# Decode attention with a gated mixer on one core: a shorter TensorE program and a hand-ordered first part

## The chip, the core and the metric

One core of one Trainium2 chip. A core has TensorE (matrix products into PSUM), VectorE, ScalarE and GpSimd, and 16 DMA engines that move data between HBM and SBUF; SyncE issues most of the loads here. The metric is device time in microseconds of one launch, lower is better. Before the change, three runs gave a median of 193.45 us (193.33 to 193.55).

## What is computed

One token `x` of 512 numbers, 32 heads of 128, and for each head the last 4096 keys and values of a cache of 32768. Cut to what matters:

```python
xn = layernorm(x)
q  = (xn @ wq) per head                     # wq: 512 x 4096
p  = softmax(q . K[last 4096] * 128**-0.5)  # per head
s  = concat(p @ V[last 4096]) @ wo          # wo: 4096 x 512
h  = gelu(layernorm(xn) @ w1)
hs = concat(shifted h) @ w2                 # one token: every shift pads with zero, so hs = 0 @ w2
x1 = xn + hs
B  = x1 + gelu(layernorm(x1) @ w3) @ w4     # w3: 512 x 1376, w4: 1376 x 512
out = x + s * silu(B)
```

All is in bf16. K and V together are 67.1 MB, wq and wo 8.4 MB, w2 to w4 3.3 MB; the rest is small.

## The kernel before

**Groups.** Heads go in 8 groups of G = 4. A group's keys are one load of 128 partitions x 128 rows x 128 (4 MB): partition 4b + a holds rows of head a. A loop over steps s = 0 to 9 (from line 531) loads K of group s and V of group s - 2, computes scores of group s, the softmax of group s - 1 and the output of groups s - 2 and s - 3. K has three buffers, V has two, and the V buffers lie where the first part's weights were, so the first V load waits until those are read. Loads stand in a fixed order on SyncE's queue (`load`, line 75; w2, w3, w4, K0 in two halves, K1, K2, V0, K3, V1, and so on; last V7 in chunks of 64, 32 and 32 rows, then four heads of wo). wq and x are loaded by ScalarE's queue.

**Scores in two ways.** Of the 128 key rows per partition, `nd(g)` rows go to VectorE (`k_vector`, whose product is line 321 and whose sum is line 323): a product with the broadcast q, then a sum over 128, in four parts. The others go to TensorE: `k_turn` transposes pairs of rows as fp32 (line 339), ScalarE copies the result (line 342), `k_scores` multiplies by q (line 350). `nd` is 64 for groups 0 and 7 and 80 for the others.

**Softmax.** `sm_max`, `sm_turn`, `sm_exp` (lines 361 to 389) find each head's maximum and take the exponentials with a running sum on ScalarE. `sm_den` and `sm_rden` (lines 391 to 399) add the sums over the partitions by a product with ones and invert them, once for each group.

**Values.** `v_wide` (line 423) is 32 products for each group; `v_turn` and `v_add` turn and sum the result, `v_out` multiplies by the inverse denominator. The last group's final 32 rows go through `v_part` (line 458, products at 461). `ox_spread`, `ox_pick`, `y_wide` and `y_head` multiply the outputs by wo. `warm(n)` (line 504) issues n products of zeros whose result nobody reads.

**First part** (lines 182 to 280): layer norms, `hs` as 16 products with w2 (line 233), q as 32 products (line 208) with its broadcast `q_bc` and transposes, the input of the gelu in 20 products (line 252), three transposes of it (line 258), 15 products into `hr_ps` (line 270), and the gate `g_row`. Before the change a scheduler orders these instructions on each engine; from line 529 on, TensorE, VectorE and ScalarE are in a `manual_schedule`, which keeps them in the order of the program text. PSUM tiles of the tag `misc` have one buffer, of `sT` two, of `pt` three.

The lines of the main loop that the change touches:

```python
            elif s > 1:
                sm_den(s - 2)
                sm_rden(s - 2)
...
            y_wide(1, False)
            sm_den(NG - 2)
            sm_rden(NG - 2)
            y_wide(0, False)
            warm(3)
            v_wide(h, v)
            sm_den(NG - 1)
            sm_rden(NG - 1)
```

Of the kernel before, what the change touches and what calls it, by code (L numbers as in the profile page):

```python
# [8 lines left out]
P = 128  # L9
# [17 lines left out]
def kernel(  # L27
# [120 lines left out]
    def rows_open(ps):  # L148
        nc.tensor.matmul(ps[:], lhsT=zero_bf[:], rhs=ident_bf[:], start=True, stop=False,
                         skip_group_check=True)  # L150
# [30 lines left out]

    x_f = small.tile([P, KC], FP32, name="x_f")
# [16 lines left out]

    q_row = wts.tile([P, H // G, 2, Dh], BF16, name="q_row")  # L200
    q_bc = small.tile([P, H // G, Dh], BF16, name="q_bc")
    qr = [ps_tr.tile([P, 4, Dh], FP32, tag="pt", name="qr_ps") for _ in range(2)]
    for b in range(2):
        zeros(qr[b][:])
        for c in range(KC):
            wc = wq_sb[:, c, :].rearrange("p (g a d) -> p g a d", a=G, d=Dh)
            for a in range(G):
                nc.tensor.matmul(qr[b][32 * a:32 * a + 1], lhsT=xq_bf[:, c:c + 1], rhs=wc[:, 4 * b:4 * b + 4, a, :],  # L208
                                 start=False, stop=(c == KC - 1), skip_group_check=True)
    nc.scalar.copy(out=q_row[:, 0:4, 0, :], in_=qr[0][:])  # L210
    nc.vector.tensor_copy(out=q_row[:, 4:8, 0, :], in_=qr[1][:])  # L211
    for b in range(2):
        qb_ps = ps_tr.tile([P, 4, Dh], FP32, tag="pt", name="qb_ps")
        nc.tensor.matmul(qb_ps[:], lhsT=sel[:].rearrange("k b a -> k (b a)"), rhs=q_row[:, 4 * b:4 * b + 4, 0, :],
                         start=True, stop=True)
        nc.scalar.copy(out=q_bc[:, 4 * b:4 * b + 4, :], in_=qb_ps[:])
# [11 lines left out]
    shifted_bf = small.tile([P, KC], BF16, name="shifted_bf")  # L228
    nc.vector.memset(shifted_bf[:], 0.0)
    hs_ps = ps_misc.tile([P, KC], FP32, tag="misc", name="hs_ps")  # L230
    for j in range(KC):
        for c in range(KC):
            nc.tensor.matmul(hs_ps[:, j:j + 1], lhsT=w2_sb[:, c, j::4],
                             rhs=shifted_bf[:, c:c + 1], start=(c == 0), stop=(c == KC - 1))
    x1_f = small.tile([P, KC], FP32, name="x1_f")
    nc.vector.tensor_tensor(out=x1_f[:], in0=xn_f[:], in1=hs_ps[:], op=ALU.add)
    xc3, _, rstd3 = ln_stats(x1_f[:], "z3")
    z3_bf = small.tile([P, KC], BF16, name="z3_bf")
    nc.vector.tensor_scalar(out=z3_bf[:], in0=xc3[:], scalar1=rstd3[:], scalar2=None, op0=ALU.mult)

    xn_row = small.tile([P, P], FP32, name="xn_row")
    nc.vector.tensor_scalar(out=xn_row[:], in0=x_row[:], scalar1=negmean[:], scalar2=rstd[:],
                            op0=ALU.add, op1=ALU.mult)

    a_ps = ps_misc.tile([P, 3, P], FP32, tag="misc", name="a_ps")
    zeros(a_ps[:])
    for c in range(KC):
        wc = w3_sb[:, c, 0:10 * P].rearrange("p (q r) -> p r q", r=10)
        parts = [(j, a_ps[32 * j:32 * j + 1, :, :], wc[:, 3 * j:3 * j + 3, :]) for j in range(3)]
        parts += [(3, a_ps[96:97, 0, :], wc[:, 9, :]), (3, a_ps[96:97, 1, 0:96], w3_sb[:, c, 10 * P:F])]  # L250
        for j, dst, w in parts:
            nc.tensor.matmul(dst, lhsT=z3_bf[:, c:c + 1], rhs=w, start=False, stop=(c == KC - 1),
                             skip_group_check=True)
    a_row = wts.tile([P, 3, P], BF16, name="a_row")
    nc.scalar.activation(out=a_row[:], in_=a_ps[:], func=ACT.Gelu_apprx_tanh)  # L255
    at_ps = ps_misc.tile([P, 3, P], BF16, tag="misc", name="at_ps")
    for m in range(3):
        nc.tensor.transpose(at_ps[:, m, :], a_row[:, m, :], ident_bf[:])
    a_bf = small.tile([P, 3, 4], BF16, name="a_bf")
    nc.vector.tensor_copy(out=a_bf[:], in_=at_ps[:, :, 0:P:32])  # L260

    hr_ps = ps_misc.tile([P, KC, P], FP32, tag="misc", name="hr_ps")
    zeros(hr_ps[:])
    terms = [(shifted_bf[:, c:c + 1], w2_sb[:, c, :]) for c in range(KC)]
    for i in range(11):
        n = P if i < 10 else 96
        terms.append((a_bf[0:n, i % 3, i // 3:i // 3 + 1], w4_sb[0:n, i, :]))
    for i, (col, w) in enumerate(terms):
        r = 32 * (i % 4)
        nc.tensor.matmul(hr_ps[r:r + 1].rearrange("r j n -> r (j n)"), lhsT=col, rhs=w, start=False,  # L270
                         stop=(i >= len(terms) - 4), skip_group_check=True)
# [10 lines left out]

    make_masks(16)
    make_masks(8)
    make_masks(4)

    y_ps = ps_y.tile([P, P], FP32, name="y_ps")
    rows_open(y_ps)  # L290

# [16 lines left out]
    def nd(g):  # L308
        return 64 if g == 0 or g >= LATE else 80
# [68 lines left out]
    def sm_exp(g):  # L378
        s = st[g]
        mb_ps = ps_misc.tile([P, G], FP32, tag="misc", name="mb_ps")  # L380
        nc.tensor.matmul(mb_ps[:], lhsT=par_t[:].rearrange("k b a -> k (b a)"), rhs=md[:], start=True,  # L381
                         stop=True)
        mb = sm_pool.tile([P, G], FP32, tag="mb", name="mb")
        nc.scalar.copy(out=mb[:], in_=mb_ps[:])  # L384
        s["pT"] = sm_pool.tile([P, CP, G], BF16, tag="pT", name="pT")
        s["sum"] = sm_pool.tile([P, G], FP32, tag="sum", name="sum")
        for a in range(G):
            nc.scalar.activation(out=s["pT"][:, :, a], in_=s["S"][:], func=ACT.Exp, scale=scale,  # L388
                                 bias=mb[:, a:a + 1], accum_out=s["sum"][:, a:a + 1])

    def sm_den(g):
        s = st[g]
        s["den"] = ps_misc.tile([P, G], FP32, tag="misc", name="den_ps")
        nc.tensor.matmul(s["den"][:], lhsT=ones_f[:], rhs=s["sum"][:], start=True, stop=True)  # L394

    def sm_rden(g):
        s = st[g]
        s["rden"] = sm_pool.tile([P, G], FP32, tag="rden", name="rden")
        nc.vector.reciprocal(out=s["rden"][:], in_=s["den"][:])  # L399
# [64 lines left out]
    def v_out(g):  # L464
# [5 lines left out]
        if g >= NG - 5:  # L470
            nc.vector.tensor_tensor(out=o_blk[b][:, c:c + G], in0=st[g]["oT"][:], in1=st[g]["rden"][:],
                                    op=ALU.mult)
            return
# [48 lines left out]
    def y_head(h):  # L522
# [4 lines left out]
    region = tc.manual_schedule(engines={mybir.EngineType.PE, mybir.EngineType.DVE,  # L527
                                         mybir.EngineType.Activation})
    region.__enter__()
    v_pool = None  # L530
    for s in range(NG + LAG):
# [22 lines left out]
        if s < NG:  # L554
# [11 lines left out]
            if s == 7:  # L566
                v_turn(h - 1)
                v_add(h - 1)
                v_out(h - 1)
            elif s > 1:  # L570
                sm_den(s - 2)
                sm_rden(s - 2)
            elif s == 1:
                sm_max(0)
            k_vector(s, kn, 1)
            keys(2, 4)
            if s == 7:
                sm_den(h)
                sm_rden(h)
# [38 lines left out]
        elif s == NG:  # L618
# [4 lines left out]
            sm_den(NG - 2)  # L623
            sm_rden(NG - 2)
            y_wide(0, False)
            warm(3)
            v_wide(h, v)
            sm_den(NG - 1)
            sm_rden(NG - 1)
# [19 lines left out]
    region.__exit__(None, None, None)  # L649
    y = small.tile([P, P], FP32, name="y")  # L650
# [34 lines left out]
```

## Time and profile before

| what | value |
|---|---|
| time, median of three runs | 193.45 us |
| span of the profiled execution (first to last instruction) | 191.2 us |
| TensorE matmul busy | 116.4 us (61%), 1159 instructions |
| TensorE weight loads busy | 74.2 us (39%), 1159 instructions |
| VectorE busy | 150.9 us (79%) |
| ScalarE busy | 89.2 us (47%) |
| DMA | 79.02 MB, mean 413 GB/s |
| mean granted TensorE clock | 0.720 |

The page gives no total for the profiled execution beyond its span; the median of the runs is 2.25 us longer than the span. The span's rows of slices cut it into 40 equal pieces of 4.78 us: a digit is the busy share in tenths, PEclk the granted share of TensorE's clock. A load's "us to landing" runs from its issue, so it holds the time in the queue. In a timeline row the first number is the start in us from the span's start, the second how long the merged instructions took, and the bracket tells how long the engine was idle before and which event ended that. Matmul ends are modelled.

### The profile page before, as it was taken

How to read it: one execution, taken by the hardware profiler on the slowest of the kernel's cores; microseconds unless marked ns; L12 is line 12 of the kernel's file. 1: busy time of each engine (PE TensorE's matmuls, PEld its weight loads, DVE VectorE, ACT ScalarE, POOL GpSimd, SP SyncE). 2: the span in 40 equal slices, each digit the busy share in tenths (PEclk: the TensorE clock that was granted, in tenths of full speed). 3: DMA queues.
4: the chain of work that ended last, by engine and by line, in shares of the span. 5: the costliest groups of instructions: out<-in, count | busy, mean ns of one | idle time of the engine just before them, and what ended most of it. 6: DMA issues, size and time to landing. Idle time of an engine off the chain costs nothing.

```text
span 191.2 us, 2839 instructions
## 1 busy us (share of the span) xinstructions
PE 116.4 (61%) x1159; PEld 74.2 (39%) x1159; DVE 150.9 (79%) x175; ACT 89.2 (47%) x191; POOL 2.3 (1%) x11
## 2 busy tenths in 40 slices
PE   1653754989825368256845772680888189739762
PEld 0430222767614334143334441540763077313322
DVE  1660159979999999999999999999999999980111
ACT  2001370888794076427464564542475148733120
POOL 2110000000000000000000000000000000000000
PEclk9999695555755557955695588557567858975998
DMA  6999999999999999999999999999999998999990
GB/s 211 447 430 404 431 418 439 439 439 437 432 434 439 432 429 432 432 439 432 422 432 432 418 422 418 452 439 435 439 432 434 435 432 372 471 425 405 420 371 32
DMA packets 4572, 79.02 MB, mean 413 GB/s; under 512 B 624, under 2 KB 1232, under 8 KB 1488
## 3 DMA queue, kind: packets, MB, share of 16 engines
q1 hardware_dynamic: 4264, 74.65, 91.6%
q10 hardware_dynamic: 296, 4.20, 5.1%
q8 instruction: 9, 0.15, 0.3%
q14 instruction: 3, 0.02, 0.0%
HBM read 78.84 MB, written 0.00 MB: 412 GB/s over the span
## 4 chain that ended last, share of the span: by engine, by line
DVE 46%; DMA 43%; PE 5%; ACT 3%; issue 1%; SPq 1%; ACTq 0%; DVEq 0%
DMA kv<-in_A_k_cache_dram 31%; DVE S L323 28%; DVE prod L321 15%; DMA kv<-in_A_v_cache_dram 10%; ACT kt L342 3%; DMA x_bf<-in_A_x_dram 2%; PE pt L339 2%; PE ov L427 1%; DVE m L366 1%; DVE S L364 1%; SPq L76 1%; PE sT L350 1%; DVE mx L374 1%; PE oT L461 1%; PE ot_ps L444 0%
## 5 line engine op out<-in xcount | busy, mean ns | idle before, releaser
L323 DVE TENSOR_REDUCE S<-prod 128x20 f32<-128x2560 bf16 (+1 forms) x32 | 86.0, 2686 | 1.1
L342 ACT COPY kt<-pt 128x1024 bf16<-128x1024 bf16 x52 | 51.2, 1013 | 40.4 <-PE pt L339 38.7
L339 PE MATMUL pt<-ident_f,kv 128*128 128x128 f32 x208 | 46.7, 376 | 10.8 <-DMA kv<-in_A_k_cache_dram 10.8
L321 DVE TENSOR_TENSOR prod<-kv,q_bc 128x2560 bf16<-128x2560 bf16 (+1 forms) x32 | 45.4, 1418 | 3.9 <-DMA kv<-in_A_k_cache_dram 3.7
L339 PEld LDWEIGHTS pt<-ident_f,kv 128*128 128x128 f32 x208 | 34.2, 196 | 14.4 <-DMA kv<-in_A_k_cache_dram 10.5
L350 PE MATMUL sT<-q_pair,kt 128*128 128x8 bf16 x416 | 19.4, 170 | 15.7 <-ACT kt L342 15.5
L350 PEld LDWEIGHTS <-kt 128*128 128x128 bf16 x416 | 16.4, 104 | 26.8 <-ACT kt L342 25.8
L427 PE MATMUL ov<-kv,pT 128*16 128x512 bf16 x248 | 22.0, 515 | 1.4 <-DMA kv<-in_A_v_cache_dram 1.4
L388 ACT ACTIVATE pT<-S,mb 128x128 bf16<-128x128 f32 x32 | 13.9, 573 | 0.3
L372 PE MATMUL mt_ps<-ident_f,m 128*1 128x128 f32 x8 | 2.9, 359 | 17.4 <-DVE rden L399 16.9
L433 ACT COPY ov_sb<-ov 128x512 f32<-128x512 f32 x8 | 4.7, 586 | 17.1 <-PE ov L427 17.1
L427 PEld LDWEIGHTS <-pT 128*16 128x16 bf16 x248 | 6.9, 109 | 13.2 <-issue 11.4
L359 ACT ACTIVATE own<-sT,par 128x48 f32<-128x48 f32 (+1 forms) x32 | 7.5, 356 | 3.7 <-PE sT L350 3.7
L444 PE MATMUL ot_ps<-ident_f,ov_sb 128*128 128x128 f32 x32 | 7.1, 359 | 2.9 <-ACT mb L384 1.9
L211 DVE CAST q_row<-qr_ps 128x512 bf16<-128x512 f32 x1 | 0.7, 692 | 9.9 <-PE qr_ps L208 9.9
L388 ACT ACTIVATION_READ_ACCUMULATOR pT<-S,mb 128x1 f32 x32 | 8.3, 258 | 0.0
L372 PEld LDWEIGHTS mt_ps<-ident_f,m 128*1 128x1 f32 x8 | 0.6, 80 | 17.9 <-DVE rden L399 17.2
L399 DVE RECIPROCAL rden<-den_ps 128x4 f32<-128x4 f32 x8 | 1.4, 175 | 7.0 <-PE den_ps L394 7.0
L381 PE MATMUL mb_ps<-md,par_t 5*128 5x4 f32 x16 | 3.9, 311 | 4.1 <-DVE md L376 4.1
L255 ACT ACTIVATE a_row<-a_ps 128x384 bf16<-128x384 f32 x1 | 0.5, 491 | 12.0 <-remote 12.0
L444 PEld LDWEIGHTS ot_ps<-ident_f,ov_sb 128*128 128x128 f32 x32 | 4.5, 178 | 3.9 <-ACT mb L384 2.3
L208 PE MATMUL qr_ps<-wq_sb,xq_bf 128*1 128x512 bf16 x32 | 3.1, 566 | 3.7 <-DMA wq_sb<-in_A_wq_dram 3.7
(122 smaller groups left out, 81.6 us busy)
## 6 DMA issues: line engine op xcount, KB each, us to landing
kv<-in_A_k_cache_dram SPq DMA_DIRECT2D x7, 4096.0 KB, 31.3
kv<-in_A_v_cache_dram SPq DMA_DIRECT2D x7, 4096.0 KB, 30.6
wq_sb<-in_A_wq_dram ACTq DMA_DIRECT2D x1, 4096.0 KB, 17.6
kv<-in_A_k_cache_dram SPq DMA_DIRECT2D x2, 2048.0 KB, 27.4
wo<-in_A_wo_dram SPq DMA_DIRECT2D x1, 2048.0 KB
kv<-in_A_v_cache_dram SPq DMA_DIRECT2D x1, 2048.0 KB
kv<-in_A_v_cache_dram SPq DMA_DIRECT2D x2, 1024.0 KB, 17.6
w_sb<-in_B_w_dram SPq DMA_DIRECT2D x1, 1376.0 KB, 9.1
```

Source lines behind the costliest of these rows:

```text
L321: nc.vector.tensor_tensor(out=prod[:, 0:m, :], in0=kn[:, rows, :], in1=q_bc[:, g:g + 1, :].to_broadcast([P, m, Dh]), op=ALU.mult)
L323: nc.vector.tensor_reduce(out=st[g]["S"][:, rows], in_=prod[:, 0:m, :], axis=AX.X, op=ALU.add)
L339: nc.tensor.transpose(pt[:, i, :], kn[:, c:c + 2, :].rearrange("p c d -> p (c d)").bitcast(FP32), ident_f[:])
L342: nc.scalar.copy(out=kts[b][:, 0:n, :], in_=pt[:, 0:n, :].bitcast(BF16))
L350: nc.tensor.matmul(st[g]["sT"][:, c:c + 2, :].rearrange("p c a -> p (c a)"), lhsT=kt[:, i, l::2], rhs=q_pair[:, g, l, :], start=(l == 0), ...
L359: nc.scalar.mul(s["own"][:, 0:m, a], s["sT"][:, 0:m, a], par[:, a:a + 1])
L372: nc.tensor.transpose(mt_ps[:], s["m1"][:], ident_f[:])
L381: nc.tensor.matmul(mb_ps[:], lhsT=par_t[:].rearrange("k b a -> k (b a)"), rhs=md[:], start=True, stop=True)
L388: nc.scalar.activation(out=s["pT"][:, :, a], in_=s["S"][:], func=ACT.Exp, scale=scale, bias=mb[:, a:a + 1], accum_out=s["sum"][:, a:a + 1])
L427: nc.tensor.matmul(ov[r:r + 4 * G], lhsT=s["pT"][:, c:c + 4, :].rearrange("p i a -> p (i a)"), rhs=v[:, c:c + 4, :], start=(i < 4), stop=( ...
L433: nc.scalar.copy(out=s["ov_sb"][:], in_=ov[:])
L444: nc.tensor.transpose(ot_ps[:, step * j:step * j + P], s["ov_sb"][:, j, :], ident_f[:])
```

## The change

Seven edits, in the order of the program:

- `manual_schedule` for TensorE and ScalarE now begins before the first part, so that these two run it in the written order; VectorE's region begins where all three did.
- `hs` is made as a row: four products of 512 columns into `hr_ps` (now a tile of the tag `sT`), a ScalarE copy of the row, four transposes of one row. `hr_ps` keeps the four products, so the later sum with w4 has 11 products instead of 15.
- The gelu's input takes 4 products per chunk of w3 instead of 5, in another column layout; two fp32 transposes of pairs instead of three bf16 ones, placed between the two q broadcasts.
- The opening of `y_ps` and the z3 layer norm move ahead of the q products on TensorE.
- Denominators are made in pairs of groups, one product and one inversion for two, at steps 3, 5 and 7 and after the second-last V.
- Group 0 has 80 rows on VectorE instead of 64, so 48 on TensorE.
- `warm(3)` ahead of the second-last `v_wide` is gone.

In the built program of each, TensorE has 1779 rows before and 1691 after (an fp32 product counts as one row there); SyncE's order of loads and what they wait for is the same. VectorE's order in the first part differs by the mask steps, which come before the sum `x1` after the change. ScalarE loads a table for its first copy, then one for the gelu.

```diff
+    order = tc.manual_schedule(engines={mybir.EngineType.PE, mybir.EngineType.Activation})
+    order.__enter__()
...
+    hr_ps = ps_s.tile([P, KC, P], FP32, tag="sT", name="hr_ps")
+    zeros(hr_ps[:])
...
+    for c in range(KC):
+        hr_add(0, shifted_bf[:, c:c + 1], w2_sb[:, c, :], False)
+    hs_row = wts.tile([1, D], FP32, name="hs_row")
+    nc.scalar.copy(out=hs_row[:], in_=hr_ps[0:1].rearrange("p j n -> p (j n)"))
     hs_ps = ps_misc.tile([P, KC], FP32, tag="misc", name="hs_ps")
     for j in range(KC):
-        for c in range(KC):
-            nc.tensor.matmul(hs_ps[:, j:j + 1], lhsT=w2_sb[:, c, j::4],
-                             rhs=shifted_bf[:, c:c + 1], start=(c == 0), stop=(c == KC - 1))
+        nc.tensor.transpose(hs_ps[:, j:j + 1], hs_row[0:1, j::4], ident_f[0:1, 0:1])
...
-        parts = [(j, a_ps[32 * j:32 * j + 1, :, :], wc[:, 3 * j:3 * j + 3, :]) for j in range(3)]
-        parts += [(3, a_ps[96:97, 0, :], wc[:, 9, :]), (3, a_ps[96:97, 1, 0:96], w3_sb[:, c, 10 * P:F])]
+        parts = [(a_ps[32 * j:32 * j + 1, 0:n], wc[:, 2 * j:2 * j + n]) for j, n in enumerate((2, 2, 1))]
+        parts += [(a_ps[96:97, 0, 0:96, 0], w3_sb[:, c, 10 * P:F])]
...
-    for m in range(3):
-        nc.tensor.transpose(at_ps[:, m, :], a_row[:, m, :], ident_bf[:])
+        for m in range(2):
+            nc.tensor.transpose(at_ps[:, m, :], a_row[:, m].rearrange("p q l -> p (q l)").bitcast(FP32), ident_f[:])
...
     for b in range(2):
+        if b == 1:
+            a_turn()
         qb_ps = ps_tr.tile([P, 4, Dh], FP32, tag="pt", name="qb_ps")
...
     def nd(g):
-        return 64 if g == 0 or g >= LATE else 80
+        return 64 if g >= LATE else 80
...
     def sm_den(g):
-        s = st[g]
-        s["den"] = ps_misc.tile([P, G], FP32, tag="misc", name="den_ps")
-        nc.tensor.matmul(s["den"][:], lhsT=ones_f[:], rhs=s["sum"][:], start=True, stop=True)
+        den = ps_misc.tile([P, 2 * G], FP32, tag="misc", name="den_ps")
+        nc.tensor.matmul(den[:], lhsT=ones_f[:], rhs=st[g - 1]["sums"][:], start=True, stop=True)
+        rden = sm_pool.tile([P, 2 * G], FP32, tag="rden", bufs=2, name="rden")
+        nc.vector.reciprocal(out=rden[:], in_=den[:])
+        for i in range(2):
+            st[g - 1 + i]["rden"] = rden[:, G * i:G * i + G]
...
-            elif s > 1:
+            elif s in (3, 5):
                 sm_den(s - 2)
-                sm_rden(s - 2)
...
             y_wide(1, False)
-            sm_den(NG - 2)
-            sm_rden(NG - 2)
             y_wide(0, False)
-            warm(3)
             v_wide(h, v)
             sm_den(NG - 1)
-            sm_rden(NG - 1)
```

## The prediction

> **What bounds the kernel.** I read the page first: how full the DMA engines are over the span, and the chain that ended last.
>
> ```profile
> PEclk9999695555755557955695588557567858975998
> DMA  6999999999999999999999999999999998999990
> GB/s 211 447 430 404 431 418 439 439 439 437 432 434 439 432 429 432 432 439 432 422 432 432 418 422 418 452 439 435 439 432 434 435 432 372 471 425 405 420 371 32
> ...
> q8 instruction: 9, 0.15, 0.3%
> ```
>
> The 16 DMA engines are full from the second slice to the last but one, at 420 to 440 GB/s, while no compute engine is full throughout (VectorE 79%). The stretches agree: 426, 431, 434, 426, 436 and 418 GB/s for 2.5-30, 30-60, 60-90, 90-120, 120-150 and 150-186.3 us. The kernel is a stream of 79 MB with work hung on it. The chain of work calls VectorE 46% of the path, but its last long piece is a load (second column: us):
>
> ```profile
> 167.79 18.54 DMA kv<-in_A_v_cache_dram
> 186.33 0.05 issue
> 186.38 0.97 PE oT L461 x32
> 187.35 0.02 issue
> 187.37 0.17 DVE o L471
> 187.55 0.04 issue
> 187.59 0.42 PE y_ps L155 x16
> ```
>
> Does the stream ever run dry? The timeline of the issuing queue answers: the last V is issued here (three DMAs, 166.55), and the V before it still occupies the engines until about 176.
>
> ```profile
> 166.55 1.83 SPq L76 DMA_DIRECT2D kv<-in_A_v_cache_dram  x3
> 168.43 1.10 SPq L76 DMA_DIRECT2D wo_rows<-in_A_wo_dram  x2
> ```
>
> Bytes say the same earlier: 4.19 MB at 430 GB/s take 9.75 us; adding loads up in order, each is issued 8 to 29 us before its turn. A buffer that comes free 2 us later delays nothing. Third, the timeline of TensorE at the end (idle before each, and its releaser, in brackets):
>
> ```profile
> 175.56 1.07 PE L507 MATMUL wm<-zero_bf 128*128 128x512 bf16 x3
> 176.56 1.90 PE L427 MATMUL ov<-kv,pT 128*16 128x512 bf16 x32
> 181.50 1.04 PE L427 MATMUL ov<-kv,pT 128*16 128x512 bf16 x16 [1.02 <-DMA kv<-in_A_v_cache_dram]
> 183.93 0.61 PE L427 MATMUL ov<-kv,pT 128*16 128x512 bf16 x8 [0.41 <-DMA kv<-in_A_v_cache_dram]
> 185.81 0.40 PE L155 MATMUL y_ps<-y_sum,ind 128*1 128x128 f32 x8
> 186.38 0.96 PE L461 MATMUL oT<-pT,kv 128*128 128x4 bf16 x32 [0.17 <-DMA kv<-in_A_v_cache_dram]
> ```
>
> TensorE waits for each of the last three V chunks: 1.02, 0.41 and 0.17 us. Its slack is about 1.4 us up to the second chunk, and only 0.17 us between second and third. After 186.33 the rest (4.86 us to the end of the span, 191.2) is fixed work. So the time is: when the last V chunk lands, plus 4.86, plus what lies outside the span (median 193.45 less span 191.2 = 2.25 us). The bytes, the order of the loads and the tail's instructions are not edited.
>
> **The change, part by part.**
>
> *hs as a row.* Out: 16 products, 0.67 us (at 7.28). In: one opening product (0.4), four of 512 columns (0.39, the row at 25.38), a ScalarE copy (0.59, as the 128x512 copies), four one-row transposes (0.4 by the 0.37 us transpose of m): 1.8 us, so +1.1. ScalarE also loads a table more, 1.28 us by the row at 2.96; in the built order it comes before the gelu, while ScalarE sits idle until 16.2. VectorE's twelve mask steps now stand before the sum: they run while hs_row is made, at most +1. The gelu products ended at 16.17, so they end by 19.5; the q products wait for wq until 19.91 (3.74 us of idle, releaser: DMA). Cost 0; without that cover, 1 to 3 us of early TensorE time, and still none at the end, since the stream runs on.
>
> *Gelu input in 16 products, two transposes, hr without its own four products.* Same columns (1376 per chunk), so about the old 2.92 us. The two transposes now stand between the two q broadcasts: 0.55 us by the row of ot_ps (1.09 for four). VectorE's first keys come 0.5 later at worst, 25.6 instead of 25.1, but they wait for K until 26.09. Cost 0.
>
> *80 rows of first keys on VectorE.* Four times (1.49 - 1.23) + (2.82 - 2.29) = +3.16 us. The row at 41.91 waited 0.99 us for K1, so group 1 starts 2.2 later. Groups 1 to 5 run without a gap (41.91 to 133.6); two reciprocals fewer on them give back 0.2. Group 6 waited 0.55 for K6: +1.4. A third reciprocal (0.1) and 0.36 us of idle before mx in group 7 leave about +0.9 at the last softmax: mb at 172.7 instead of 171.8. ScalarE loses two copies (1.01 each) and TensorE two batches in group 0, both idle later anyway. The K buffers come free up to 2.2 us later, against at least 8 us of lead: cost 0.
>
> *Paired denominators.* Four of eight products (0.36 to 0.59) and four reciprocals (0.17) go. The added waits: v_out of groups 4 and 6 now waits for a sum made with the next group's. For 4, the product stands right behind v_turn (157.1) and VectorE comes there at 158.8; for 6, the exponentials end near 175.3, and v_out came at 180.1. The next keys queue behind the first of these waits on VectorE. Between 0 and 0.6 us there, by the product's own row; I take 0, since VectorE arrives later.
>
> *No warm(3) before the second-last V.* Out: 1.07 us. y_wide's 24 products (1.02 + 1.88) now run in one piece from 173.2 to 176.1. V6 lands only near 176.5: its completion packets end at 176.13, and the last chunk's ended 0.41 before TensorE saw it (185.92, 186.33). v_wide then starts at 176.5, as before. The filler stood on a wait. Next late is V7's first chunk, at 181.50, unchanged.
>
> The clock is where a rule speaks against this edit. The windows give 0.50 for 172.7-176.1 (busy 3.40 of 3.40 us) and 1.00 from 176.1. The Trainium skill, "TensorE: Matmul & The Clock Gate", section "HAM oscillation — how this bites in real kernels", asks for no gap over about 3.4 us, and its section "What's actually happening" has the clock rise only after a busy window of that length. By the row the real products fill 173.2-176.1 and 176.5 on, so the clock comes as before: 0. By the rule a window with a gap in it may not count: v_wide runs cold, 3.52 us (the 32 at 70.38) instead of 1.90, +1.6 against 1.4 of slack: +0.2 to 0.4. I take 0.
>
> *The shorter program itself.* The q8 row counts nine fetches of 16 KB. In the trace's packets they start at 27.7, 47.2, 69.1, 91.8, 111.2, 130.7, 150.0, 175.3 and 187.1 us: one per some 250 TensorE instructions, on one DMA engine each, 1.0 to 1.1 us long. The Trainium skill, "Runtime: NRT & Kernel Launch", section "Instruction fetch mechanics", calls crossing such a block mostly hidden. The packets disagree. Each load ends with one completion packet per engine. For K0's second half 15 engines end between 29.92 and 30.41 and one at 31.67, after the first fetch. Each later fetch moves another engine back by 1.1 to 1.6, and the last chunk ends on its engines between 183.93 and 185.92. So 2.0 us of lag, of which about 0.5 is there without fetches, sit in the end. By the rule 105 fewer instructions are worth nothing. By the packets a fetch is worth up to 1.5 us if it leaves the latest engine alone. Which case is this? At 175.3 some 270 instructions are left. Most of the 105 go ahead of that point, so the same fetch comes with some 170 left, at V7's first chunk (181.5): later, but before the last chunk is through. The ninth only disappears, and it lay behind the last chunk (187.1). The other seven stay, and one of them left an engine at 1.94 against 1.99. Gain 0.05 at most; I take 0.
>
> Sum: 191.2 + 0 - 0.05 to 191.2, plus 2.25: 193.4.
>
> **Rivals.**
>
> *Slower: a cold array at the end.* Without the filler the clock stays at 0.5 through the last chunks. Behind the second chunk: eight products 0.61 to 0.88, four transposes 0.66 to 1.09, eight y products 0.40 to 0.60 (the row at 30.48): +0.90, less 0.17 of slack, +0.73. Behind the third: oT's 32 by the score products (0.38 cold, 0.36 warm for eight) +0.1, at most +0.96; the heads +0.2. About +1.0: 194.5. It decides once the clock is not up by 182.9. For it: windows at half clock although busy (139 us); against: 6 us of dense 512-column products, and before that the clock came at once. With the milder +0.2 to 0.4: 193.8.
>
> *Faster: fetches fall elsewhere.* If the engine a fetch lands on changes with the program's length, the lag may be 1.5 on a prompt engine: -0.45, 193.0; if none sat on a late engine, -1.5, 191.95. For it: 2.0 us of lag are real. Against: eight fetches come before the end in either program. By the same means two on one engine would cost up to +1.5, but no two did so before.
>
> *The change does nothing for time:* the forecast itself.
>
> **Chances.** A measurement of this kernel can tell about 0.2% (0.39 us) from no change. Unchanged 0.50 (own range 193.1 to 193.8); faster, by fetches or a smoother stream, 0.27 (about 192.8); slower, by the clock or two fetches on one engine, 0.23 (about 194.2). The range 192.5 to 194.4 leaves out the extremes of both, some 0.2.
>
> **What would show it.** Right: the GB/s row again near 430; the last load landing within 0.4 us of 186.3 with TensorE waiting for it; group 1 on VectorE starting near 44; v_wide at 176.5 with the clock at 1.00 soon after; eight fetches by then, one near 181. Wrong: TensorE or ScalarE last before oT, a gap in the DMA row, or completion packets of the last chunk far from 2.0 us apart.

## The result and the profile after

The changed kernel took 194.5 us (median of 8 runs, 193.69 to 195.34) beside 193.46 us for the kernel before on the same chip (8 runs, 193.33 to 193.95). The ratio is 1.0051 with a 95% interval of 1.0033 to 1.007: about 1.0 us slower, where 193.4 was forecast. The times also spread over 1.65 us, against 0.62 before. The profiled execution is the shortest of the eight, 193.69 us, with a span of 191.9; so 1.8 us lie outside the span, where before it was about 2.2.

The page of the changed kernel first: the granted clock, the share and the rate of the DMA engines in 40 slices, and the fetches of TensorE's program.

```profile
PEclk9999975555555555855699558557655855695798
DMA  6999999999999999999999999999999998999990
GB/s 206 450 438 404 412 427 434 437 437 439 427 439 437 430 430 427 430 437 430 430 434 437 417 430 400 437 437 437 430 434 432 437 437 377 466 430 396 406 367 23
...
q8 instruction: 8, 0.13, 0.3%
```

The stream is as full as before, and there are eight fetches instead of nine, as foretold (the eighth at 180.7 us in the trace's packets, forecast about 181.5). Nothing in these rows says that a microsecond was lost. The chain of work does (second column: us):

```profile
178.34 2.67 PE ov L436 x31
181.03 0.59 ACT ov_sb L442
...
183.00 0.97 PE ov L436 x16
...
187.12 0.95 PE oT L470 x32
188.09 0.17 DVE o L480
```

Before, the last long piece was the load of the last V. It is not on this chain any more: the chain's shares were DVE 46% and DMA 43%, and are DVE 74%, PE 11% and DMA 9%. TensorE's timeline of the end says the same, by what is missing:

```profile
175.61 2.73 PE L527 MATMUL yr_ps<-wo,ox 128*1 128x512 bf16 x24
178.12 2.85 PE L436 MATMUL ov<-kv,pT 128*16 128x512 bf16 x32
...
182.93 1.04 PE L436 MATMUL ov<-kv,pT 128*16 128x512 bf16 x16
...
184.78 0.60 PE L436 MATMUL ov<-kv,pT 128*16 128x512 bf16 x8
...
187.11 0.94 PE L470 MATMUL oT<-pT,kv 128*128 128x4 bf16 x32
```

None of the products on the three V chunks has a bracket; before, they waited 1.02, 0.41 and 0.17 us. `v_wide` of group 6 starts at 178.12 instead of 176.56 and takes 2.85 us instead of 1.90, since the clock is at half until 180.05. The last products start at 187.11 instead of 186.38. TensorE's 1.4 us of slack are gone.

In this run, the shortest of the eight, they are only just gone. The weight load (PEld) of the last products, which goes ahead of them, still waited for the last chunk, which the chain above, going by the products, does not show:

```profile
187.04 0.92 PEld L470 LDWEIGHTS <-kv 128*128 128x128 bf16 x32 [0.22 <-DMA kv<-in_A_v_cache_dram]
```

Before, it waited for that chunk too and started at 186.37. So here the last V landed some 0.67 us later, and this is nearly all by which the span is longer (191.9 for 191.2). In a longer run it is TensorE that comes late (e18 below).

Where was TensorE's slack used up? Its step of group 7, before:

```profile
156.01 1.09 PE L444 MATMUL ot_ps<-ident_f,ov_sb 128*128 128x128 f32 x4
...
159.28 0.36 PE L394 MATMUL den_ps<-sum,ones_f 128*128 128x4 f32 x2
...
161.54 0.27 PE L372 MATMUL mt_ps<-ident_f,m 128*1 128x128 f32 x1
```

and after, TensorE, then VectorE:

```profile
156.41 1.09 PE L453 MATMUL ot_ps<-ident_f,ov_sb 128*128 128x128 f32 x4
159.40 0.60 PE L404 MATMUL den_ps<-sum,ones_f 128*128 128x8 f32 x2 [1.89 <-DVE oT L459]
...
164.76 0.37 PE L381 MATMUL mt_ps<-ident_f,m 128*1 128x128 f32 x1
```

```profile
159.13 0.21 DVE L459 TENSOR_REDUCE oT<-ot_ps 128x4 f32<-128x64 f32 x1
...
165.18 0.28 DVE L383 TENSOR_REDUCE mx<-mt_ps 1x4 f32<-1x128 f32 x1 [1.28 <-PE mt_ps L381]
```

TensorE stands idle for 1.89 us ahead of the denominator product, and the event that ends it is VectorE's `v_add`. `den_ps` and `ot_ps` share the one PSUM buffer of the tag `misc`, so the product could not start until `v_add` had read `ot_ps`. Before, two batches of keys stood between the two, and nobody waited. Now all the keys of group 7 queue behind the product. `mt_ps` comes 3.2 us later than before (about half of it by this wait: 163.11 in e1 below, which differs by the product's place alone), VectorE waits for it, and the 3.3 us are still there at the last softmax (`mb_ps` 175.12 instead of 171.79).

A second thing shows only in the packets. A load ends with one completion packet for each DMA engine. The first engine ended the third and last chunk of the last V at 183.93 before and at 184.52 after (the expectations of e13, e14 and e17 call the same packet the second chunk's). No load was issued too late for its turn; each took a little longer.

### The profile page after: what moved, and what is told of

It reads as the page before. It is cut to its first block, busy times and chain, and to the rows that moved or that the text cites. A ratio compares the mean times of both kernels' runs of the same rounds, so it can differ in the third digit from the quotient of the medians.

```text
span 191.9 us, 2730 instructions
## 1 busy us (share of the span) xinstructions
PE 116.6 (61%) x1107; PEld 73.4 (38%) x1107; DVE 154.4 (80%) x171; ACT 89.6 (47%) x191; POOL 2.3 (1%) x11
## 4 chain that ended last, share of the span: by engine, by line
DVE 74%; PE 11%; DMA 9%; issue 2%; ACT 2%; POOL 1%; ACTq 1%; DVEq 0%; POOLq 0%
DVE S L332 45%; DVE prod L330 23%; DMA wq_sb<-in_A_wq_dram 9%; PE pt L348 2%; PE ov L436 2%; PE yr_ps L527 2%; DVE m L375 1%; DVE S L373 1%; PE qr_ps L261 1%; DVE mx L383 1%; PE ot_ps L453 1%; DVE md L385 1%; ACT q_row L273 1%; PE sT L359 1%; PE oT L470 0%
## 5 line engine op out<-in xcount | busy, mean ns | idle before, releaser
L332 DVE TENSOR_REDUCE S<-prod 128x20 f32<-128x2560 bf16 (+1 forms) x32 | 88.1, 2753 | 1.1
L351 ACT COPY kt<-pt 128x1024 bf16<-128x1024 bf16 x50 | 49.3, 1013 | 32.5 <-PE pt L348 30.9
L330 DVE TENSOR_TENSOR prod<-kv,q_bc 128x2560 bf16<-128x2560 bf16 (+1 forms) x32 | 46.4, 1450 | 3.8 <-ACT q_row L273 3.5
L359 PE MATMUL sT<-q_pair,kt 128*128 128x8 bf16 x400 | 18.8, 170 | 13.7 <-ACT kt L351 13.6
L436 PE MATMUL ov<-kv,pT 128*16 128x512 bf16 x248 | 23.4, 540 | 0.0
L390 PEld LDWEIGHTS mb_ps<-md,par_t 5*128 5x128 f32 x16 | 3.8, 291 | 17.1 <-issue 13.5
L393 ACT COPY mb<-mb_ps 128x4 f32<-128x4 f32 x8 | 1.3, 163 | 16.2 <-PE mb_ps L390 16.2
L406 DVE RECIPROCAL rden<-den_ps 128x8 f32<-128x8 f32 x4 | 0.8, 202 | 7.0 <-PE den_ps L404 7.0
```

Source lines behind the costliest of these rows:

```text
L330: nc.vector.tensor_tensor(out=prod[:, 0:m, :], in0=kn[:, rows, :], in1=q_bc[:, g:g + 1, :].to_broadcast([P, m, Dh]), op=ALU.mult)
L332: nc.vector.tensor_reduce(out=st[g]["S"][:, rows], in_=prod[:, 0:m, :], axis=AX.X, op=ALU.add)
L351: nc.scalar.copy(out=kts[b][:, 0:n, :], in_=pt[:, 0:n, :].bitcast(BF16))
L359: nc.tensor.matmul(st[g]["sT"][:, c:c + 2, :].rearrange("p c a -> p (c a)"), lhsT=kt[:, i, l::2], rhs=q_pair[:, g, l, :], start=(l == 0), ...
L436: nc.tensor.matmul(ov[r:r + 4 * G], lhsT=s["pT"][:, c:c + 4, :].rearrange("p i a -> p (i a)"), rhs=v[:, c:c + 4, :], start=(i < 4), stop=( ...
```

## The experiments

Four suspects: the early denominators, the 80 rows, the missing filler, and the slower stream. For the last, the built program gives the start of each tile in SBUF. The paired tiles (two of 8 numbers instead of three of 4, for `sum` and for `rden`) moved the tiles behind them, up to 64 bytes down (each has a place of 32 bytes, and there are two fewer), so the V buffers start at 159936 and 192704 instead of 160000 and 192768. That is a remainder of 192 by 256 instead of 0. The first part's weights and the last wo rows, which lie behind `sm` too, moved with them. The K buffers stay at a remainder of 128.

All runs in one table. "Late" is the denominators moved behind the second pair of key batches, "V" the remainder of the V buffers by 256 bytes. The kernel before, run beside them, had medians from 193.34 to 193.45.

| run | what it is | V | median, us | lowest to highest | ratio to before, 95% |
|---|---|---|---|---|---|
| e1 | after + late | 192 | 193.74 | 193.52-194.18 | 1.0007-1.002 |
| e2 | before + pairs | 192 | 193.86 | 193.57-194.9 | 1.0016-1.0041 |
| e3 | before + 80 rows | 0 | 194.62 | 193.03-195.76 | 1.0035-1.0074 |
| e4 | before without filler | 0 | 193.38 | 193.11-194.96 | 0.9986-1.0014 |
| e5 | after + V back | 0 | 193.63 | 192.81-195.36 | 1.0003-1.0041 |
| e6 | before + V moved | 192 | 194.21 | 194.20-194.31 | 1.0031-1.0055 |
| e7 | before + pairs, late, V back | 0 | 193.02 | 192.69-193.39 | 0.9967-0.9987 |
| e8 | after + late, V back, 64 rows | 0 | 193.15 | 192.66-194.96 | 0.9989-1.0029 |
| e9 | e8 + filler | 0 | 193.19 | 192.8-194.15 | 0.9974-0.9998 |
| e10 | e7 + 80 rows | 0 | 193.87 | 192.82-194.38 | 1.0003-1.0024 |
| e11 | e7 without filler | 0 | 193.05 | 192.78-194.98 | 0.9968-1.0008 |
| e12 | e7 + 8 tiny products | 0 | 192.96 | 192.73-193.26 | 0.996-0.9984 |
| e13 | e7, V at 0 by 512 | 0 | 192.99 | 192.74-193.66 | 0.9968-0.9986 |
| e14 | e7, V at 128 | 128 | 193.69 | 193.49-193.91 | 1.0002-1.002 |
| e15 | e7, K at 0 | 0 | 192.99 | 192.56-195.46 | 0.9957-0.9986 |
| e16 | after + late, V back | 0 | 192.97 | 192.75-193.12 | 0.9959-0.9977 |
| e17 | e16, K at 0 | 0 | 192.89 | 192.51-202.41 | 0.9965-0.999 |

### The denominators: e1, e2

```diff
# e1, against the changed kernel, step 7
                 v_add(h - 1)
-                sm_den(h)
-                v_out(h - 1)
...
             keys(2, 4)
             if s == 7:
+                sm_den(h)
+                v_out(h - 1)
                 keys(4, nb - 2)
```

> The changed kernel with one move: in the step of group 7 the paired denominator of groups 4 and 5 and v_out(4) stand after the second pair of key batches instead of right behind v_turn and v_add. Theory A (TensorE waits there 1.89 us for VectorE's v_add, because den_ps and ot_ps share the one PSUM buffer of tag misc, and the keys of group 7 queue behind it): no wait of den_ps for v_add, mt of group 6 back from 164.8 to about 162.5, mb of the last softmax back from 175.1 to about 173.2, v_wide before the last V from 178.1 to about 176.6, ratio to before near 1.000 (0.999 to 1.002). Theory B (the missing filler leaves TensorE's clock low at the end): ratio stays near 1.005, runs stay spread over 1 us and more. Theory C (VectorE's 80 rows alone): most of the loss stays, 1.003 or more.

Measured 193.74. The product ran at 159.68 without a wait, `mt_ps` came at 163.11, and the spread fell from 1.65 us to 0.66. The last products again wait for the last load (0.17 us, at 187.03). Two of the expected signs did not come: `mb_ps` of the last softmax is at 175.00 and `v_wide` of group 6 at 177.99, nearly as in the changed kernel, because `v_wide` of group 5 ran at half clock here (3.59 us for 1.90). The profiled span is 191.9, as there. So the move took away the long runs and left the short ones as they were, and what is left of the loss is the stream.

e2 makes the paired denominators alone in the kernel before.

> The kernel before with the paired denominators alone. Theory A: the wait of den_ps for v_add is there but short, 0.4 to 0.8 us, since VectorE is not late without the 80 rows (v_add at 157.5, the transposes end at 157.1): ratio 1.000 to 1.002. If pairing alone made the loss, 1.004 or more. Theories B and C: 1.000.

Measured 193.86. The wait is there, 0.61 us instead of 1.89, since without the 80 rows VectorE comes earlier. The last chunk's first engine ended at 184.61: the pairs alone bring the slower stream too.

### The rows and the filler alone: e3, e4

```diff
# e3, against the kernel before
-        return 64 if g == 0 or g >= LATE else 80
+        return 64 if g >= LATE else 80
```

> The kernel before with 80 rows of group 0 on VectorE alone. Theory A: VectorE 1.4 us later at group 7, mb of the last softmax near 172.7 (before 171.8), no new wait of TensorE, filler still there: ratio 1.000 to 1.001. Theory C: 1.003 to 1.005.

Measured 194.62, with a spread of 2.7 us: alone, the 80 rows cost about as much as the whole change. The profile is of the shortest run, 193.03; there VectorE's reciprocal holds `mt_ps` by 1.35 us, and `mb_ps` comes at 173.83. No profile shows one of the long runs.

e4 is the kernel before without `warm(3)` ahead of the second-last `v_wide`.

> The kernel before without the three filler products alone. Theory A: v_wide before the last V starts when V6 lands (176.5), ratio 1.000. Theory B: the clock is granted one window later in some runs, spread of runs over 0.5 us, ratio 1.001 to 1.005.

Measured 193.38, within the error of before: 12 of 13 runs at 193.11 to 193.53, one at 194.96. In the profiled run `v_wide` of group 6 ran at half clock (3.36 us), and the time was 193.4 all the same.

### The place of the V buffers: e5, e6, e13, e14

```diff
# e5, against the changed kernel (an unused tile of 64 bytes; e6: 448 bytes in the kernel before)
+    sm_pool.tile([P, 32], BF16, tag="fill", bufs=1, name="fill")
     def sm_turn(g):
```

> The changed kernel with an unused tile of 64 bytes per partition in the pool sm, which puts the V buffers back at 160000 bytes (as before; the paired tiles had moved them and all first weights to 159936). Theory D (V's place costs the stream 0.65 us): the shortest span goes from 191.9 back to 191.2, the last V chunk's first engine ends near 183.9 instead of 184.5; TensorE's lateness is untouched, so the runs still spread up to 193.5 and the median falls by 0.2 to 0.6: ratio 1.001 to 1.004. Without D: 1.005 as the changed kernel.

> The kernel before with an unused tile of 448 bytes in the pool sm and nothing else: V's buffers start at 160448, which has the same remainder by 512 as in the changed kernel (192, before 256). Theory D: the shortest span goes from 191.1 to 191.8, ratio 1.003 to 1.004, runs no more spread than before. Without D: 1.000.

e6 runs the kernel before, instruction for instruction, with V 448 bytes higher: 194.21 us, five runs within 0.11. The place alone costs 0.8 us (of the V buffers and of what lies behind them). e5 gives the changed kernel its old place back: 193.63, but still up to 195.36, since the early denominators are still in it. e13 and e14 ask which property of the address matters, in the version e7 below.

> The version that took 193.02 (before with paired denominators, made late) with the V buffers at a remainder of 0 by 512 bytes (160256 and 193024) instead of 256. If a start at a multiple of 256 is what the stream wants: 193.0 again, and the last V's second chunk lands on its first engine near 183.9. If only a multiple of 512 is the best: faster, up to 0.8 us, 192.2 to 192.8. If the one place was lucky: 193.8, with the chunk near 184.6.

> The same with the V buffers at a remainder of 128 (160384 and 193152). If a start at a multiple of 256 is what the stream wants: as slow as the remainder of 192, so 193.7 to 193.9 and the second chunk near 184.6. If any multiple of 128 serves: 193.0 and 183.9.

A multiple of 256 is enough (e13, 192.99), and 128 is as bad as 192 (e14, 193.69). By the completion packets (first engine, one profiled run each):

| kernel | V, K remainder by 256 | K1 takes | V0 landed to last chunk landed, 17 loads | a chunk of 1 MB | last chunk landed |
|---|---|---|---|---|---|
| before | 0, 128 | 9.72 | 124.89 | 2.45 | 183.93 |
| e13 | 0, 128 | 9.72 | 124.91 | 2.45 | 184.01 |
| e16 | 0, 128 | 9.70 | 124.89 | 2.45 | 183.92 |
| after | 192, 128 | 9.71 | 125.35 | 2.48 | 184.52 |
| e6 | 192, 128 | 9.72 | 125.26 | 2.48 | 184.58 |
| e14 | 128, 128 | 9.70 | 125.36 | 2.48 | 184.55 |
| e15 | 0, 0 | 9.68 | 124.85 | 2.45 | 183.80 |

The price is nearly the same for each load, whatever its size: 0.03 us on a chunk of 1 MB, and 0.37 to 0.47 us over 17 loads, 0.022 to 0.028 each. A load of K or V has 128 rows, one for each partition, of 8 to 32 KB. The K loads between the V loads share in it (9.71 us instead of 9.69), though their own place is the same; why is open. Whether the first part's weights, which lie in the same space, cost more ahead of V0 doesn't show clearly: from the first load to V0 it took 55.33 to 55.43 us in the first three kernels of the table and 55.34 to 55.57 in the next three.

The Trainium skill, "DMA: Bandwidth & Descriptors", section "How a descriptor splits into AXI transactions", has a rule that may bear on it: a descriptor that doesn't start at a multiple of 256 bytes begins at the boundary below, and the unused bytes ahead of its start are fetched and cost beats of 32 bytes too. An estimate by that page: 192 bytes ahead of an 8 KB row are 6 beats on 256 (2.3%), 128 bytes are 4 (1.6%); on a 32 KB row 0.6% and 0.4%. Measured are 0.03 of 2.45 us (1.2%) and 0.03 of 9.69 (0.3%). So the direction, the independence of the row's length and the order of size agree. But 128 costs as much here as 192, and the page speaks of bytes fetched, while here it is the written side, in SBUF, that moved. The measurement decides; the mechanism is not shown.

### Late pairs in their place: e7, and each suspect put back into it: e10, e11, e12

e7 is the kernel before with paired denominators, made late, and with V at 160000.

> The kernel before with the paired denominators alone, the one of groups 4 and 5 and v_out(4) after the second pair of key batches, and 64 bytes of unused tile, so V lies as before. Theories A and D together: no wait of den_ps for v_add, the span back at 191.1 without the runs up to 193.1 that the pairs alone had; the time outside the span, 2.2 before and 1.8 with the pairs, stays at 1.8: ratio 0.998 (0.997 to 0.999). If pairing costs something else too: 1.001 or more.

Measured 193.02: 0.23% faster than before (ratio 0.9977), no run above 193.39. The span is hardly shorter (190.9 to 191.6; profiled before, 191.2); 1.8 instead of 2.2 us lie outside it.

> The kernel before with paired denominators, these late, the V buffers in their old place, and 80 rows of group 0 on VectorE as in the change; the filler is there. It differs from the version that took 193.02 by the 80 rows alone. Theory (the 80 rows bring the last softmax about 2 us later, so TensorE has no slack at the end and the time hangs on the clock): median 193.5 to 194.3, with runs from 192.8 up to 195. Rival (80 rows are hidden as the prediction had it): 193.0, no run above 193.5.

Measured 193.87. TensorE's timeline of a run of 194.17:

```profile
174.67 2.73 PE L520 MATMUL yr_ps<-wo,ox 128*1 128x512 bf16 x24
177.34 1.46 PE L509 MATMUL wm<-zero_bf 128*128 128x512 bf16 x3
178.72 2.74 PE L429 MATMUL ov<-kv,pT 128*16 128x512 bf16 x32
```

With 80 rows TensorE comes so late that V6 is already there, and the filler now stands in the way: 1.46 us at half clock. The last products start at 187.60, without waiting for a load.

> The version that took 193.02 (before, with paired denominators made late and V in its old place) without the filler of three products ahead of the second-last v_wide. Theory (the filler keeps TensorE busy while the clock's window runs; without it v_wide runs cold where the phase is bad): a second group of times near 194.6 in some of the runs (between 1 in 13 and 1 in 3, the shares of two earlier kernels without the filler), the others near 192.9; median 192.9 to 193.3. Rival (the filler does nothing here): all runs 192.6 to 193.4, median 192.95.

Measured 193.05; 12 of 14 runs up to 193.35, two at 194.87 and 194.98. A profile of a short run:

```profile
172.64 1.78 PE L520 MATMUL yr_ps<-wo,ox 128*1 128x512 bf16 x24
176.45 3.59 PE L429 MATMUL ov<-kv,pT 128*16 128x512 bf16 x32 [2.04 <-DMA kv<-in_A_v_cache_dram]
```

With 64 rows and no filler TensorE stands idle for 2.04 us, and `v_wide` then runs at half clock. It is just in time in this run: the weight load of the last products still waits 0.22 us for the last V. What happened in the two long ones no profile shows.

> The version that took 193.02 with eight products of one column of zeros more on TensorE, ahead of the first keys (16 TensorE instructions more in the trace, under 1 us, at a place where TensorE waits for K). It tests the time outside the span, which was 2.15 us before and with 6 instructions fewer, and 1.8 us in all kernels with 16 or more fewer. If it is the length of TensorE's program: the span stays 190.9 to 191.6 and the time outside goes back to 2.1 to 2.2, so the median is about 193.35. If it is something else in the edit: outside stays 1.8, median 193.0.

Measured 192.96, and 1.75 to 1.86 us outside the span. So the time outside is not set by the number of TensorE's instructions, which e12 has as before (1159 products in both traces).

### The changed kernel mended: e8, e9, e16

> The changed kernel with three edits undone: the denominator of groups 4 and 5 and v_out(4) later, 64 rows of group 0 on VectorE, V's buffers at 160000. What is left is the hand-made first part, the paired denominators and no filler. If theories A, C and D name all that was lost: span 191.1, ratio 0.998 (0.996 to 0.999). If the first part or the shorter program loses too: 1.001 or more.

Measured 193.15 in two clusters: 14 runs from 192.66 to 193.4, 8 from 194.53 to 194.96. Here all was taken back but the first part, the pairs and the missing filler. The same instability as in e11, in 8 of 22 runs.

> The changed kernel with its denominators late, 64 rows of group 0 on VectorE, the V buffers back at 160000 and 192768 bytes, and now the filler of three products ahead of the second-last v_wide again (only the hand-made first part and the pairs are left of the change). Theory (without the filler v_wide of group 6 runs cold in about a third of the runs): no run above 193.6, median near 193.0 and ratio about 0.998; the second group of times near 194.6 that the same kernel had without the filler is gone. Rival (the two groups come from the hand-made first part, whose shorter program shifts the clock's windows): times near 194.6 stay in a third of the runs.

Measured 193.19; the cluster near 194.6 is gone (13 of 14 runs up to 193.64, one at 194.15). `v_wide` took 2.04 us in its profile. So with 64 rows the filler does its work.

e16 leaves the 80 rows and the missing filler as the change has them, and mends only the other two.

> The changed kernel with its denominators late and the V buffers at 160000 and 192768; it still has 80 rows of group 0 on VectorE and no filler. If the 80 rows and the missing filler cost what they did alone (the rows brought 193.02 to 193.87, the missing filler made some runs 1.8 longer): median 193.4 to 194.0, spread from 192.8 to 195. If they cost nothing once the other two are mended: 193.0, and the whole loss was the place of V and the early denominators.

Measured 192.97, all 14 runs within 0.37 us, ratio 0.9968: the lowest ratio in the table. Its timeline (TensorE):

```profile
159.22 0.59 PE L406 MATMUL den_ps<-sum,ones_f 128*128 128x8 f32 x2 [0.25 <-DVE oT L461]
...
175.16 2.73 PE L529 MATMUL yr_ps<-wo,ox 128*1 128x512 bf16 x24
177.67 2.22 PE L438 MATMUL ov<-kv,pT 128*16 128x512 bf16 x32
...
186.28 0.96 PE L472 MATMUL oT<-pT,kv 128*128 128x4 bf16 x32 [0.17 <-DMA kv<-in_A_v_cache_dram]
```

`y_wide` ends when V6 is there, `v_wide` follows with no gap, and the last products again wait for the load. My expectation that each would cost what it cost alone was wrong: the 80 rows fill the place where the filler stood. Two pairs of runs differ by these rows alone. Without the filler they took the cluster near 194.6 away (e8 to e16); with the filler they cost 0.85 us (e7 to e10, both with the first part as before; the changed first part with rows and filler was not run).

### The K buffers too: e15, e17

> The same with the K buffers moved from a remainder of 128 to 0 by 512 (16896, 49664, 82432), the V buffers at a remainder of 256. If a buffer that does not start at a multiple of 256 slows its loads, K pays what V paid: 0.7 to 0.9 us less in the stream, the last chunk earlier by as much, time 192.1 to 192.5. If the place matters for V alone, or 128 is as good as 0: 193.0.

> The changed kernel with its denominators late, the V buffers at a remainder of 256 by 512 bytes, and the K buffers at 16896, 49664 and 82432 (remainder 0) instead of 128. It differs from the kernel that took 192.97 by the K buffers' place. If K pays for its place: the last V's second chunk on its first engine near 183.80 instead of 183.92 and a median of 192.8 to 192.9, all runs under 193.2. If it doesn't: 192.97, 183.9.

K1 took 9.68 us instead of 9.70 to 9.72, and the lowest times are the lowest of all (192.56 and 192.51; the eight kernels with V in place, late pairs and K at 128 have 192.66 to 192.82). But the medians moved by 0.08 at most, and both kernels had long runs (one of 195.46 in e15, three from 196.0 to 202.41 in e17), where the kernel before also had one of 199.28. Some 0.1 us of gain is likely; it is not shown.

### A long run of the changed kernel: e18

> The changed kernel once more, for its profile. If a long run (over 194.8) is a cold array at the end, the 8 products of the second chunk take 0.88 us or more instead of 0.60 and the clock is at half when the last chunk starts; if it is work ahead of the chunks, v_wide of group 6 takes 3.5 us instead of 2.85, the 16 products of the first chunk start after 183.5 instead of 182.93, and the last products still run at 0.95. If the run is a short one (193.7 to 194.2), it shows the first profile again and settles nothing.

This run took 194.98 us, with a span of 193.2 (the kernel before, once, 194.01). Its timeline of TensorE:

```profile
168.54 3.59 PE L436 MATMUL ov<-kv,pT 128*16 128x512 bf16 x32
...
176.59 0.55 PE L390 MATMUL mb_ps<-md,par_t 5*128 5x4 f32 x2 [0.65 <-DVE md L385]
...
184.22 1.04 PE L436 MATMUL ov<-kv,pT 128*16 128x512 bf16 x16
...
188.40 0.94 PE L470 MATMUL oT<-pT,kv 128*128 128x4 bf16 x32
```

Up to 168.5 it is the short run's timeline, with the wait at the denominators 1.84 instead of 1.89. Then `v_wide` of group 5 takes 3.59 us where the short run had 1.90: the clock was at half from 153.85 to 181.15, and in the short run at full from 166.40 to 173.22. `mb_ps` comes at 176.59 instead of 175.12, and 1.3 to 1.5 us are carried to the end. The last products take 0.94 us in both: the array is not cold at the end. Nor did `v_wide` of group 6 take 3.5 us; it took 2.67. The stream was the same (last chunk at 184.51), and this time the weight load of the last products, at 188.34, did not wait for it: TensorE is 1.3 us later than in the short run.

e1 shows what the early product adds to such a run. There `v_wide` of group 5 ran at half clock as well, but with the product late `mb_ps` came at 175.00 instead of 176.59, and the last products still met the last V. So this long run came of both together, the wait at the denominators and a `v_wide` at half clock. It is the only long run of this kernel that was traced.

## Why the prediction was wrong

**Paired denominators: a step that failed.** It read "For 4, the product stands right behind v_turn (157.1) and VectorE comes there at 158.8; [...] I take 0, since VectorE arrives later." I asked whether VectorE would wait for the product. It is the product that waits for VectorE, through the shared PSUM buffer, with the keys of group 7 behind it. Both times were in the prediction, 1.7 us apart; TensorE was idle for 1.89 us. Mended with V in place, the time falls from 193.63 (e5) to 192.97 (e16), so the step cost 0.66 us of the median and most of the spread. It is the 80 rows that make VectorE so late: without them the wait was 0.61 us, and the early product cost about 0.2 us (193.86 in e2, and 193.69 in e14 with the product late and V at a remainder of 128).

**When the last V lands: the other step that failed.** It read "The bytes, the order of the loads and the tail's instructions are not edited", which was so, and the sum kept the landing where it was. But the tiles that were resized in one pool shifted the buffers of another, and each load took some 0.03 us longer. From e1 (193.74) to e16 (192.97) this costs 0.77 us.

**The sum.** The four medians, with both edits as changed, each mended, and both:

| | V at 192 | V at 0 |
|---|---|---|
| product early | 194.5 | 193.63 (e5) |
| product late | 193.74 (e1) | 192.97 (e16) |

V's place costs 0.77 to 0.87 us, the early product 0.66 to 0.76. The medians come from different sets of runs, and that of e5 is uncertain by 0.4 us. They nearly add, but in the profiled runs the two do not add: each alone already brings the last products to 187.03 (e1) or 187.14 (e5), and both together to 187.11. It is the long runs that make the medians differ. Mended of both, the changed kernel takes 192.97, 0.49 less than before's 193.46. Of this gain about 0.4 is time outside the span, and 0.1 is within the scatter of the medians.

**80 rows.** The start of group 1 on VectorE was right (44.21 for "near 44"), and so was +1.4 us at group 7 (`v_add` at 158.95 in e16, 157.53 before). The term "+0.9 at the last softmax" was mis-sized: in e16 `mb_ps` came at 174.67 instead of 171.79, +2.9. VectorE's 1.4 us held `mt_ps`, this pushed `v_wide` of group 5 to 166.62 (164.60 before), and there it ran at half clock, 3.59 instead of 1.90: the clock was at half from 154.43 to 178.33, where before it was at full from 159.02 to 169.26. VectorE then waited 1.44 us for `ot_ps`, which stands behind `v_wide`, and 1.4 + 1.44 is nearly all of the 2.9. So the delay was not carried on at its own size. K's lead was right: every load followed the one before without a gap.

**No filler.** "Cost 0" came out for the kernel as changed, but not by the argument given, which was that y_wide would end at 176.1 and leave a gap. It ends near 178, after V6 has landed. Where there is a gap (e4, e8, e11), `v_wide` ran at half clock in the profiled run, 3.36 to 3.59 us, as the prediction's case "by the rule" had it (3.52). The gap did not take the clock down. In e11 it fell at 173.66, within y_wide, and stayed at half until 180.48; TensorE was busy for 1.37 of the 3.41 us from 173.66. In e9, with the filler, it was busy for 3.03 of the 3.41 us from 173.44, and the clock was back at 176.85. So the gap kept the clock down for one step more. These three profiled runs are short ones (193.05 to 193.40): a `v_wide` at half clock was just in time in them.

**First part and fetches.** Cost 0 for both edits of the first part: VectorE's first keys came at 26.14 instead of 26.09 (the profile names ScalarE's copy of q as the last wait, not K). e9 and e7 differ by the first part alone: 193.19 and 193.02, with intervals that overlap. Eight fetches before the end, and the engines' lag at the last chunk 1.97 us for 2.0: right.

**Rivals.** "A cold array at the end" gave 194.5, the measured median, but its mechanism is not what happened, so the number is luck: the last chunks ran at full clock in both profiles, and e18, a long run, was long because of `v_wide` two groups earlier, behind the early product. "Fetches fall elsewhere": they came at other times (the second at 51.0 us instead of 47.2), but the lag at the end stayed, so there was nothing to gain.

**Open.** Why 1.8 instead of 2.2 us lie outside the span. e4 (6 TensorE instructions fewer than before) and e6 (none) keep 2.1 to 2.2, all other variants have 1.74 to 1.97, e12 with its eight extra products included. And what a long run of e3, e8 or e11 looks like was not caught.

## What to carry to other kernels

When an instruction moves, list every buffer that it writes and who reads that buffer last: a shared PSUM slot is a wait that the diff doesn't show, and what queues behind it pays. When a small tile is resized, read the starts of the large load buffers from the built program again, and try them at a multiple of 256 bytes. When an engine has 1.4 us of slack, add up all delays on it along its chain before any one is called hidden, and judge edits that share that slack together: the 80 rows cost 0.85 us with the filler and nothing without it. And look at the weight loads as well as at the products before saying that an engine no longer waits for a load.

## What the hardware showed that was not expected

- The start of an SBUF buffer sets the rate of the loads into it: 2.45 us for 1 MB at a remainder of 0 by 256 bytes, 2.48 us at 128 and 192. The time went from 193.0 to 193.7 us (e13, e14), and for the kernel before from 193.4 to 194.2 (e6).
- The same 32 products took 1.90 us in one run and 3.59 us in another of the same kernel, after a start that differs by 0.2 us. In every trace here the granted clock keeps a value for 3.41 us or a multiple of it (0.5 from 173.22 to 180.05, then 1.0 to 190.29, in the changed kernel), and the points where it changes lie elsewhere in each run. The Trainium skill, "TensorE: Matmul & The Clock Gate", section "What's actually happening", calls the window free-running; that agrees. A kernel with slack on TensorE hides it: e7, with a spread of 0.7 us, had its `v_wide` of group 5 at half clock in its profile (3.58 us), and `mb_ps` came at 171.76 all the same (171.79 before).
- The time outside the span changed by 0.4 us between programs that differ in a few instructions.
